# Output sums of the second pass: from loads, VectorE additions and stores to ScalarE copies and adding DMAs

## The chip, the cores and the metric

The kernel runs on one core of one Trainium2 chip. The metric is the device time of one execution in microseconds (us). Beside a few timed runs there is one profiled execution, whose trace the rows below are from. TensorE (PE, with its weight loads PEld) does the matrix products, VectorE (DVE) and ScalarE (ACT) work on tiles, GpSimd (POOL) can do the same and can issue DMAs, SyncE (SP) issues DMAs.

## The reference

A linear attention over 8 batches, 8 heads, 576 positions and head size 64 gives x with 4608 tokens and 512 features. Behind it stands a gated product without a nonlinearity, in float32:

```python
a = x @ w_a                 # 4608 x 512  @  512 x 1536
b = x @ w_b
return (a * b @ w_out)      # 1536 x 512
```

Outputs are summed over the 1536 hidden features, so the sum can be built in pieces. The change lies in the second half only.

## The kernel before, in words

Everything is kept transposed, features on partitions and tokens along the row. Each float32 operand is split into a high and a low part (`hh`, `hl`), and each product takes three matmuls.

The 1536 hidden features are done in three passes of four slices of 128 (`SLICES`). Pass 0 (`moe_block`) runs beside the attention and puts its output sums in DRAM (`parts[0]`). Passes 1 and 2 (`later_passes`) go over the tokens in blocks `t0` of up to 1024, in halves of `W` = 512: for pass 1 the blocks start at 0, 512, 1536, 2560 and 3584, the first of 512 tokens. "Second pass" is pass 1. It adds its output to pass 0's sums and puts the result in `parts[1]`, which pass 2 reads, adds to and writes to `out`.

In a block of pass 1, `winograd` first makes the hidden features with seven products per pair of slices (the keys `w11`, `s1`, `s2`, `w12`, `s3`, `w22`, `s4`) in PSUM tiles `pa..`, `pb..`. ScalarE copies some of these out of PSUM (line 691: tiles `top`, `more`, `low`), which frees the PSUM tile for the next product; VectorE adds and multiplies. Then `outputs` makes eight output tiles of 128 features by 512 tokens, `(cc, half)` = (0,0), (0,1), (1,0), ... (3,1), each of 12 matmuls (line 917) into a PSUM tile `po`. When the last of the 12 is in, line 922 loads the old sums into one of three SBUF buffers `o`, line 923 adds on VectorE, line 924 stores. The PSUM tiles of `cc` 1 and 2 are the same banks that the next block's winograd uses (`sum_ba`, `sum_bb`, `sum_ca`, `sum_cb`), so its products into `pab`, `pbb`, `pac`, `pbc` wait until these tiles are read out.

Beside this runs the decoding of pass 2's weights (`load_factors`): raw words come by DMA (`raw_..`), ScalarE scales them (line 437), VectorE assembles them, ScalarE and VectorE split them (line 150 and 157, tiles `ws_..`), and SP stores the parts (`wd_..`, line 492). The split parts have four buffers, so a fifth cast waits for the store of the first.

Each engine takes its instructions in one order, set at build time by a scheduler that sorts instructions by modelled times and readiness. So the place of an instruction in its engine's order can move although its line did not.

Of the kernel before, what the change touches and what calls it, by code (L numbers as in the profile page):

```python
# [9 lines left out]
F32 = mybir.dt.float32  # L10
# [3 lines left out]
ALU = mybir.AluOpType  # L14
# [4 lines left out]
P = 128  # L19
# [41 lines left out]
def tile_kernel(ctx, tc, qT, km, kr, vm, vr, w_phi, w_a, w_b, w_out, out):  # L61
# [13 lines left out]
    nc = tc.nc  # L75
# [3 lines left out]
    DM, NT = out.shape  # L79
# [9 lines left out]
    dpool = ctx.enter_context(tc.tile_pool(name="dpool", bufs=1, space=DRAM))  # L89
# [5 lines left out]
    xun = [dpool.tile([DM, S], F32, name=f"xun{b}") for b in range(B)]  # L95
    den = [dpool.tile([H, S], F32, name=f"den{b}") for b in range(B)]
    rec = [dpool.tile([H, S], F32, name=f"rec{b}") for b in range(B)]
    parts = [dpool.tile([DM, NT], F32, name=f"part{i}") for i in range(2)]
    xnorm = dpool.tile([DM, NT], F32, name="xnorm")


# [52 lines left out]
    def split(hi, lo, src, eng_hi, eng_lo):  # L154

        copy(eng_hi, hi, src)
        eng_lo.tensor_tensor(lo, src, hi, op=ALU.subtract)  # L157
# [425 lines left out]
    def moe_block(j):  # L583
        p, T, pool = 0, TS[0], xpool
        xs = first_x if j == 0 else list(load_x(j, pool))
        hs = []
        late = len(pools_moe) > 1

        def sums(name):

            if not late:
                return ps_moe.tile([P, T], F32, tag="moe", name=name)
            return sum_tile(next(places), name)

        places = itertools.cycle(("aa", "ab", "ca", "cb", "ba", "bb"))
        yield
        for f in range(NFS[p]):
            if f == 1:
                for c, x_ in enumerate(xs):
                    nc.sync.dma_start(xnorm[c * P : (c + 1) * P, j * T : (j + 1) * T], x_[2])  # L600
            u = f"{p}_{j}_{f}"
            pab = {}
            for nm in "ab":
                acc = sums(f"p{nm}_{u}")
                hi, lo = (weights[(p, f, nm, part)] for part in "hl")
                k = 0
                for cc in range(NCC):
                    xh, xl = xs[cc][:2]
                    for w, x in ((hi, xh), (hi, xl), (lo, xh)):
                        nc.tensor.matmul(acc, w[:, cc * P : (cc + 1) * P], x, start=(k == 0), stop=(k == 3 * NCC - 1))  # L610
                        k += 1
                pab[nm] = acc
            h32 = pool.tile([P, T], F32, tag="h32", bufs=2, name=f"h32_{u}")
            nc.scalar.copy(h32, pab["a"])  # L614
            nc.vector.tensor_tensor(h32, pab["b"], h32, op=ALU.mult)  # L615
            hh = pool.tile([P, T], F32R, tag="hh", bufs=NFS[p], name=f"hh_{u}")
            hl = pool.tile([P, T], F32R, tag="hl", bufs=NFS[p], name=f"hl_{u}")
            split(hh, hl, h32, nc.scalar, nc.vector)
            hs.append((hh, hl))
            yield  # L620
        cols = slice(j * T, (j + 1) * T)
        dst = parts[0].rearrange("(c p) s -> p c s", p=P)[:, :, cols]
        for cc in range(NCC):
            if cc % 2 == 0:
                o = pool.tile([P, 2, T], F32, tag="o", bufs=2, name=f"o_{p}_{j}_{cc}")
            acc = sums(f"po_{p}_{j}_{cc}")
            k = 0
            for f, (hh, hl) in enumerate(hs):
                hi, lo = (weights[(p, f, "o", part)] for part in "hl")
                for w, h in ((hi, hh), (hi, hl), (lo, hh)):  # L630
                    nc.tensor.matmul(acc, w[:, cc * P : (cc + 1) * P], h, start=(k == 0), stop=(k == 3 * NFS[p] - 1))  # L631
                    k += 1
            nc.scalar.copy(o[:, cc % 2], acc)
            yield
            if cc % 2:
                nc.sync.dma_start(dst[:, cc - 1 : cc + 1], o)
# [43 lines left out]
    def sum_tile(k, name):  # L680
        return pools_moe[-1].tile([P, T2 // 2], F32, tag=f"sum_{k}", name=name)
# [200 lines left out]
    def later_passes(xin, after):  # L882

        W = T2 // 2
        blocks = []
        for p, sizes in ((1, [W] + [T2] * (NT // T2)), (2, [T2] * (NT // T2) + [W])):
            t0 = 0
            for T in sizes:
                blocks.append((p, t0, T))
                t0 += T  # L890
            assert t0 == NT
        xs = yield from factors_of_x(*blocks[0], xin)
        left, old_places = None, {}
        for at, (p, t0, T) in enumerate(blocks):
            pool = pools_late[0]
            if t0 == 0:
                mine = [(pool, "o", W, 3)] * 3
                old_places[p] = itertools.cycle(mine)
            src, dst = (t.rearrange("(c p) s -> p c s", p=P) for t in (parts[p - 1], out if p == 2 else parts[1]))
            hs, acc, done = {}, {}, {}  # L900

            def outputs(cc, half, fs, p=p, t0=t0, pool=pool, src=src, dst=dst, hs=hs, acc=acc, done=done):

                key = cc, half
                if key not in acc:
                    name = f"po_{p}_{t0}_{cc}"
                    if cc in (0, NCC - 1):
                        acc[key] = ps_moe.tile([P, W], F32, tag="moe", name=f"{name}_{half}")
                    else:
                        acc[key] = sum_tile("bc"[cc - 1] + "ab"[half], f"{name}_{half}")  # L910
                tok = slice(half * W, (half + 1) * W)
                for f in fs:
                    n = done[key] = done.get(key, 0) + 1
                    hi, lo = (weights[(p, f, "o", part)] for part in "hl")
                    for i, (w, h) in enumerate(((hi, hs[f][0]), (hi, hs[f][1]), (lo, hs[f][0]))):
                        n_ = dict(start=(n == 1 and i == 0), stop=(n == NFS[p] and i == 2))
                        nc.tensor.matmul(acc[key], w[:, cc * P : (cc + 1) * P], h[:, tok], skip_group_check=True, **n_)  # L917
                if done[key] == NFS[p]:
                    cols = slice(t0 + half * W, t0 + (half + 1) * W)
                    home, tag, n, bufs = next(old_places[p])  # L920
                    o = home.tile([P, n], F32, tag=tag, bufs=bufs, name=f"o_{p}_{t0}_{cc}_{half}")[:, :W]
                    nc.sync.dma_start(o, src[:, cc, cols])
                    nc.vector.tensor_tensor(o, acc[key], o, op=ALU.add)
                    nc.sync.dma_start(dst[:, cc, cols], o)

            nq = NFS[p] // 2
            if p == 2:
                found, first, steps, last_product = out_winograd(t0, T, pool, xin, src, dst)
            else:
                found = halves_found(p, T, f"{p}_{t0}", pool, hs)  # L930
            order = [(cc, half) for cc in range(NCC) for half in range(T // W)]
            last_of_pass = t0 + T == NT
            for q in range(nq):
                low_home = (xin, "ws", 2) if (p, q) == (2, 1) else (pool, "low", 1)
                quad = winograd(p, q, T, xs, f"{p}_{t0}_{q}", pool, low_home, found)
                for _ in range(3):
                    next(quad)
                    yield
                if q == 0 and left is not None:
                    left()  # L940
                if q > 0 and p == 2:
                    first()
                elif q > 0:
                    for key in order[: T // W]:
                        outputs(*key, range(2 * q))
                next(quad)
                after(p, last_of_pass, q)
                yield
            if at + 1 < len(blocks):
                xs = yield from factors_of_x(*blocks[at + 1], xin)  # L950
            if p == 2:
                yield from steps()
                left = last_product
                continue
            early = range(2 * nq - 2)
            for cc, half in order[T // W :]:
                if cc < NCC - 1:
                    outputs(cc, half, early)
                    yield
            for key in order[:-1]:  # L960
                outputs(*key, range(0 if key[0] == NCC - 1 else early.stop, NFS[p]))
                yield

            def left(outputs=outputs, key=order[-1], n=NFS[p], p=p, last=last_of_pass):
                outputs(*key, range(n))
                after(p, last, None)

        left()
        yield
# [147 lines left out]
```

## Time and profile before

| | |
|---|---|
| timed runs, median of 3 | 1240.02 us (1239.19 to 1242.61) |
| profiled execution, time | 1242.13 us |
| its span, first to last instruction | 1240.4 us |
| TensorE busy | 1201.7 us, 97% |
| VectorE, ScalarE busy | 84%, 56% |
| second pass | from about 697 to 983 us of the span |

The span leaves 1.7 us of the profiled execution's time outside. That execution lies 2.1 us above the median of the runs. Matmuls are pipelined: a matmul of 512 columns is listed with 0.39 us, but the next one starts 0.227 us behind it.

### The profile page before, as it was taken

To read this page: it belongs to the slowest core of one execution; us is meant where nothing else is said; L and a number is where in the kernel's file an instruction comes from. 1 tells how busy PE (TensorE), PEld (TensorE's weight loads), DVE (VectorE), ACT (ScalarE), POOL (GpSimd) and SP (SyncE) were. 2 spreads that over 40 slices of the span, in tenths; PEclk is the share of its full clock that TensorE was granted. 3 is DMA by queue.
4 is the path that set the end of the run, shared out by engine and by line. 5 is a ranking of instruction groups with operands and counts; after the bars stand their busy time and mean duration, and the time that the engine had idled before them with its cause. 6 is when DMAs were issued, how large, how long until landed. Compare 5 with 4: busy or idle time off the path is not lost.

```text
span 1240.4 us, 18131 instructions
## 1 busy us (share of the span) xinstructions
PE 1201.7 (97%) x6345; PEld 981.9 (79%) x6345; DVE 1039.2 (84%) x1742; ACT 697.0 (56%) x1322; POOL 159.8 (13%) x68
## 2 busy tenths in 40 slices
PE   7989999999999999999899999999999999999998
PEld 4556887888888888887678888888788888888887
DVE  7998889998999899887498866888898688888686
ACT  5767777787687777777344544444445253424332
POOL 3331222321331222313000000000000000000000
PEclk9998999999999999999999999999999999999999
DMA  6763343453443534423463231747489714241322
GB/s 197 205 192 112 92 132 97 127 154 95 137 123 95 153 111 118 117 69 93 127 219 111 102 116 38 250 147 253 153 290 394 242 52 153 68 160 62 128 68 86
DMA packets 125420, 174.87 MB, mean 141 GB/s; under 512 B 34640, under 2 KB 63696, under 8 KB 125328
## 3 DMA queue, kind: packets, MB, share of 16 engines
q1 hardware_dynamic: 125328, 173.71, 44.4%
q8 instruction: 50, 0.82, 0.3%
q14 instruction: 42, 0.34, 0.1%
HBM read 115.10 MB, written 58.56 MB: 140 GB/s over the span
## 4 chain that ended last, share of the span: by engine, by line
PE 53%; DVE 24%; DMA 13%; issue 4%; ACT 4%; SPq 1%; DVEq 0%; ACTq 0%
PE po L917 6%; PE pba L705 6%; PE paa L705 6%; PE pa L610 4%; PE pb L610 4%; PE po L631 4%; PE kvps L282 4%; PE poa L810 3%; PE pn L368 3%; PE pac L705 3%; PE pbc L705 3%; DMA rb<-rec 2%; DVE kel L157 2%; DMA r<-den 2%; DMA xun<-xn 2%
## 5 line engine op out<-in xcount | busy, mean ns | idle before, releaser
L348 POOL PARTITION_ALL_REDUCE mb<-p x64 | 159.6, 2525 | 423.7 <-ACT p L339 349.7
L157 DVE TENSOR_TENSOR qel<-qe,qeh 128x1152 fp32r<-128x1152 f32 x54 | 73.5, 1360 | 8.7 <-ACT qeh L150 8.6
L238 ACT ACTIVATE ke<-kd 128x512 f32<-128x512 f32 x64 | 40.6, 634 | 52.7 <-DVE kd L230 48.3
L157 DVE TENSOR_TENSOR kel<-ke,keh 128x1024 fp32r<-128x1024 f32 x50 | 67.4, 1347 | 1.0 <-ACT keh L150 1.0
L352 ACT ACTIVATE qe<-p 128x576 f32<-128x576 f32 x64 | 43.9, 685 | 42.8 <-DVE p L349 41.7
L150 ACT CAST qeh<-qe 128x1152 fp32r<-128x1152 f32 x54 | 62.7, 1161 | 0.0
L282 PE MATMUL kvps<-keh,vaug 128*65 128x256 f32 x200 | 56.4, 282 | 6.3 <-DVE kvl L312 6.3
L610 PE MATMUL pb<-xh,w_b_h 128*128 128x512 f32 x144 | 58.4, 405 | 3.5 <-DVE h L615 2.2
L631 PE MATMUL po<-hh,w_o_h 128*128 128x512 f32 x144 | 57.6, 407 | 2.4 <-DVE h L615 2.1
L610 PE MATMUL pa<-xl,w_a_h 128*128 128x512 f32 x144 | 57.9, 402 | 1.4 <-DVE xl L157 1.4
L610 PE MATMUL pa<-xh,w_a_h 128*128 128x512 f32 x144 | 58.6, 407 | 0.3 <-ACT h L614 0.3
L610 PE MATMUL pb<-xh,w_b_l 128*128 128x512 f32 x144 | 58.7, 408 | 0.0
L631 PE MATMUL po<-hl,w_o_h 128*128 128x512 f32 x144 | 57.7, 401 | 0.7 <-DVE hl L157 0.7
L610 PE MATMUL pb<-xl,w_b_h 128*128 128x512 f32 x144 | 58.2, 404 | 0.0
L610 PE MATMUL pa<-xh,w_a_l 128*128 128x512 f32 x144 | 57.6, 400 | 0.0
L631 PE MATMUL po<-hh,w_o_l 128*128 128x512 f32 x144 | 57.0, 396 | 0.0
L917 PE MATMUL po<-hl,w_o_h 128*128 128x512 f32 x144 | 56.4, 392 | 0.0
L917 PE MATMUL po<-hh,w_o_l 128*128 128x512 f32 x144 | 56.1, 389 | 0.0
L282 PE MATMUL kvps<-keh,vl 128*64 128x256 f32 x200 | 55.8, 279 | 0.0
L282 PE MATMUL kvps<-kel,vaug 128*65 128x256 f32 x200 | 55.8, 279 | 0.0
L150 ACT CAST keh<-ke 128x1024 fp32r<-128x1024 f32 x50 | 52.6, 1051 | 2.4 <-PE kvps L282 2.2
L567 DVE TENSOR_TENSOR x<-x,rb 128x512 f32<-128x512 f32 x36 | 28.1, 783 | 29.7 <-DMA rb<-rec 28.7
(339 smaller groups left out, 3855.6 us busy)
## 6 DMA issues: line engine op xcount, KB each, us to landing
x<-xnorm SPq DMA_DIRECT2D x32, 512.0 KB
o<-part SPq DMA_DIRECT2D x61, 256.0 KB
q<-in_qT SPq DMA_DIRECT2D x32, 288.0 KB
xun<-xn SPq DMA_DIRECT2D x64, 144.0 KB
xnorm<-x SPq DMA_DIRECT2D x36, 256.0 KB
part<-o SPq DMA_DIRECT2D x18, 512.0 KB
part<-o SPq DMA_DIRECT2D x36, 256.0 KB
k<-in_km SPq DMA_DIRECT2D x32, 256.0 KB
```

Of the source, the lines that this page charges most:

```text
L150: eng.copy(dst, src)
L157: eng_lo.tensor_tensor(lo, src, hi, op=ALU.subtract)
L238: nc.scalar.activation(e[:, :, 0, :], d, AF.Exp)
L282: nc.tensor.matmul(st["kv_ps", b, pr][:width, j], v_[:, j, :width], e_[:, j], start=(left == NFULL and j == 0 and n_ == 0), stop=(left == ...
L348: nc.gpsimd.partition_all_reduce(mb, p32, P, bass_isa.ReduceOp.absmax)
L352: nc.scalar.activation(e[:, 0], p32, AF.Exp)
L368: nc.tensor.matmul(pn[: D + 1, :HALF], kv_[:, 2 * j + s, :], e_[:, s, tok], **at)
L610: nc.tensor.matmul(acc, w[:, cc * P : (cc + 1) * P], x, start=(k == 0), stop=(k == 3 * NCC - 1))
L631: nc.tensor.matmul(acc, w[:, cc * P : (cc + 1) * P], h, start=(k == 0), stop=(k == 3 * NFS[p] - 1))
L705: nc.tensor.matmul(accs[to][i], w_, x_, skip_group_check=True, **at)
L810: nc.tensor.matmul(accs[to][m], w_, x_, skip_group_check=True, **flags)
L917: nc.tensor.matmul(acc[key], w[:, cc * P : (cc + 1) * P], h[:, tok], skip_group_check=True, **n_)
```

## The change

One array `part` in DRAM takes the place of the two. Pass 1 no longer loads the old sums. ScalarE copies each finished output tile from PSUM into a buffer `o`, and a DMA issued from GpSimd's queue adds the buffer to the old sums in DRAM. Pass 2 reads `part`.

```diff
-    parts = [dpool.tile([DM, NT], F32, name=f"part{i}") for i in range(2)]
+    part = dpool.tile([DM, NT], F32, name="part")
...
-        dst = parts[0].rearrange("(c p) s -> p c s", p=P)[:, :, cols]
+        dst = part.rearrange("(c p) s -> p c s", p=P)[:, :, cols]
...
-            src, dst = (t.rearrange("(c p) s -> p c s", p=P) for t in (parts[p - 1], out if p == 2 else parts[1]))
+            src, dst = (t.rearrange("(c p) s -> p c s", p=P) for t in (part, out if p == 2 else part))
...
                     o = home.tile([P, n], F32, tag=tag, bufs=bufs, name=f"o_{p}_{t0}_{cc}_{half}")[:, :W]
-                    nc.sync.dma_start(o, src[:, cc, cols])
-                    nc.vector.tensor_tensor(o, acc[key], o, op=ALU.add)
-                    nc.sync.dma_start(dst[:, cc, cols], o)
+                    nc.scalar.copy(o, acc[key])
+                    nc.gpsimd.dma_start(dst[:, cc, cols], o, accum_op=ALU.add)
```

The order of the engines moves with it. First ScalarE, at the seam between block 1536 and block 2560 of the second pass, before: the raw words of the weights for pass 2 (`raw_2_a`, `raw_3_a`, `raw_2_b`) are scaled, `more` and `low` of block 2560 are copied out of PSUM.

```order
L437 ACTIVATE w_2q_a_9733<-raw_2_a 128x512 [waits DMAHW0_49]
L437 ACTIVATE w_2q_a_9764<-raw_3_a 128x512 [waits DMAHW1_49,Activation_49]
L691 COPY more_2560_0_9896<-paa_2560_0_9889 128x512 [waits PE_49]
L691 COPY more_2560_0_9896<-pba_2560_0_9890 128x512 [waits PE_49]
L150 CAST ws_1_a_w_9818<-w_2q_a_9753 128x256 [waits DVE_49]
L150 CAST ws_1_a_w_9823<-w_2q_a_9753 128x256 [waits DMAHW5_49]
L437 ACTIVATE w_2q_b_9926<-raw_2_b 128x512 [waits DMAHW0_49,DVE_49]
L150 CAST ws_1_a_s_9843<-ws_2q_a 128x256 [waits DMAHW6_49,DVE_49]
L691 COPY low_2560_0_9897<-paa_2560_0_9889 128x512 [waits PE_49,Activation_49]
```

The same place in the changed kernel, from the copy of output (0,1) on (DMASW names a DMA of GpSimd's queue, DMAHW one of SP's):

```order
L922 COPY o_1536_0_1_9771<-po_1536_0_1_9584 128x512 [waits DMASW2_49,PE_49]
L437 ACTIVATE w_2q_a_9751<-raw_3_a 128x512 [waits DMAHW6_49]
L922 COPY o_1536_1_0_9783<-po_1536_1_0_9711 128x512 [waits DMASW3_49,PE_49]
L922 COPY o_1536_1_1_9797<-po_1536_1_1_9723 128x512 [waits DMASW4_49,PE_49,Activation_49]
L922 COPY o_1536_2_0_9816<-po_1536_2_0_9732 128x512 [waits DMASW5_49,PE_49,Activation_49]
L150 CAST ws_1_a_w_9801<-w_2q_a_9740 128x256 [waits DVE_49]
L150 CAST ws_1_a_w_9806<-w_2q_a_9740 128x256 [waits DMAHW0_49]
L922 COPY o_1536_2_1_9835<-po_1536_2_1_9742 128x512 [waits DMASW6_49,PE_49,Activation_49]
L437 ACTIVATE w_2q_b_9906<-raw_2_b 128x512 [waits DMAHW7_49,DVE_49]
L150 CAST ws_1_a_s_9825<-ws_2q_a 128x256 [waits DMAHW2_49,DVE_49]
L922 COPY o_1536_3_0_9861<-po_1536_3_0_9848 128x512 [waits DMASW7_49,PE_49,Activation_49]
L691 COPY more_2560_0_9876<-paa_2560_0_9869 128x512 [waits PE_49]
```

The copy `more` stood right behind the scaling of `raw_3_a`; now five output copies, two casts, the scaling of `raw_2_b` and another cast stand between. Each output copy from the fourth on waits for the DMA that read its buffer three outputs earlier. Behind it, in the changed kernel:

```order
L150 CAST ws_1_a_s_9820<-ws_2q_a 128x256 [waits DMAHW1_49,DVE_49]
L691 COPY more_2560_0_9876<-pba_2560_0_9870 128x512 [waits PE_49]
L150 CAST ws_1_a_s_9839<-ws_2q_a 128x256 [waits DMAHW1_49,Activation_49]
L150 CAST ws_1_a_w_9844<-w_2q_a_9775 128x256 [waits DMAHW2_49,Activation_49]
L437 ACTIVATE w_2q_b_10015<-raw_3_b 128x512 [waits DMAHW0_49,DVE_49]
L150 CAST ws_1_b_w_10161<-w_2q_b_9958 128x256 [waits DMAHW3_49,Activation_49]
L150 CAST ws_1_a_s_9865<-ws_2q_a 128x256 [waits DMAHW4_49,Activation_49]
L691 COPY low_2560_0_9877<-paa_2560_0_9869 128x512 [waits PE_49]
```

`low` moved behind four more casts and the scaling of `raw_3_b`; the last casts wait for stores (`wd_..`) of the first ones.

TensorE, at the same seam in the changed kernel, after the 12 matmuls of output (3,0), four of the products into `paa` and `pba` (key s2), one into `pab` and six into `pac`:

```order
L705 MATMUL pab_2560_0_9873<-xgl_2560_0_9660,w_0_a_w_7934 128x512
L705 MATMUL pab_2560_0_9873<-xgh_2560_0_9659,w_0_a_w_7934 128x512
L705 MATMUL pab_2560_0_9873<-xgh_2560_1_9698,w_0_a_w_7934 128x512
L705 MATMUL pbc_2560_0_9872<-xth_2560_0_9651,w_0_b_s_8045 128x512 [waits Activation_49]
L705 MATMUL pbc_2560_0_9872<-xtl_2560_0_9652,w_0_b_s_8045 128x512
L705 MATMUL pbc_2560_0_9872<-xth_2560_0_9651,w_0_b_s_8045 128x512
L705 MATMUL pbc_2560_0_9872<-xth_2560_1_9690,w_0_b_s_8045 128x512
L705 MATMUL pbc_2560_0_9872<-xtl_2560_1_9691,w_0_b_s_8045 128x512
L705 MATMUL pbc_2560_0_9872<-xth_2560_1_9690,w_0_b_s_8045 128x512
L705 MATMUL pab_2560_0_9873<-xgl_2560_1_9699,w_0_a_w_7934 128x512
L705 MATMUL pab_2560_0_9873<-xgh_2560_1_9698,w_0_a_w_7934 128x512
L705 MATMUL pbb_2560_0_9874<-xgh_2560_0_9659,w_0_b_w_8039 128x512
```

Before, `pbc` and its neighbours waited for VectorE and came behind the s3 product into `paa`; now they wait for ScalarE, and the s3 product follows the six of `pbb`. Behind it come six into `pba`, the 12 of output (3,1), four into `pab`, and then the first w22 product into `paa`, which waits for `low`.

## Rows read from the trace of the kernel before

**Rows 1.** The page of the profile: its span, and the busy time of TensorE with share and instructions.

```profile
span 1240.4 us, 18131 instructions
PE 1201.7 (97%) x6345; PEld 981.9 (79%) x6345; DVE 1039.2 (84%) x1742; ACT 697.0 (56%) x1322; POOL 159.8 (13%) x68
```

**Rows 2.** Busy time in windows of 60 us of the second pass: the window, its length, busy us and instructions of PE, PEld, DVE, ACT, POOL, granted TensorE clock, DMA share, GB/s.

```profile
700.00:760.00 60.00, 59.14 (x326) 51.44 (x326) 42.88 (x72) 25.22 (x44) 0.00 (x0) 1.00 0.31 96
760.00:820.00 60.00, 59.52 (x262) 48.81 (x262) 49.44 (x85) 25.16 (x46) 0.00 (x0) 1.00 0.51 171
820.00:880.00 60.00, 59.41 (x261) 48.31 (x259) 51.31 (x90) 24.73 (x44) 0.00 (x0) 1.00 0.60 202
880.00:940.00 60.00, 59.88 (x263) 49.34 (x264) 52.71 (x96) 26.81 (x48) 0.00 (x0) 1.00 0.73 258
```

**Rows 3.** Waits from 690 to 1000 us: who waited for what, us in total, times, longest. First those of PE, then one of ACT, then two of SP's DMA queue.

```profile
PE pba L705 <- ACT top L691: 1.1, 2, 0.6
PE paa L705 <- ACT top L691: 0.9, 1, 0.9
...
ACT more L691 <- PE paa L705: 20.2, 9, 5.3
...
SPq L924 <- DVE o L923: 25.7, 21, 6.3
SPq L922 <- DMA part<-o: 24.0, 19, 3.9
```

**Rows 4.** Costs: the VectorE additions of line 923 as a group (busy us, mean ns, idle before); ScalarE's copies of such an output tile in pass 0 and SP's issues of the loads (times, then ns minimum/median/maximum, first and last start); GpSimd's one kind of instruction.

```profile
L923 DVE TENSOR_TENSOR o<-po,o 128x512 f32<-128x512 f32 x36 | 24.3, 684 | 8.7 <-DMA o<-part 4.8 <-PE po L917 2.7 <-PE pab L705 1.1
...
L633 ACT COPY o<-po x36: 565/587/616, 162.7 to 697.2; 128x512 f32<-128x512 f32 x36
L922 SPq DMA_DIRECT2D o<-part x36: 319/320/1339, 701.4 to 976.8; - x36
...
L348 POOL PARTITION_ALL_REDUCE mb<-p x64 | 159.6, 2525 | 423.7 <-ACT p L339 349.7
```

**Rows 5.** The chain of waits at the seam between blocks 1536 and 2560: start us, length us, what. `part`, `wd_a_w` and `o` are transfers of 256 KB.

```profile
785.49 2.24 DMA part<-o
787.75 3.76 DMA o<-part
792.74 5.91 DMA wd_a_w<-ws_a_w
800.70 4.29 DMA o<-part
```

**Rows 6.** TensorE's instructions at the same seam: start us, listed us, line. 781.13 to 782.13 are the last five matmuls of output (0,0), 787.80 is the last of (2,1), 788.93 the first of (3,0), 793.47 the first s3 product into `paa`, 802.53 the first w22 product into it.

```profile
781.13 0.48 PE L917 MATMUL po<-hl,w_o_h 128*128 128x512 f32 x1
...
782.13 0.39 PE L917 MATMUL po<-hh,w_o_l 128*128 128x512 f32 x1
...
787.80 0.39 PE L917 MATMUL po<-hh,w_o_l 128*128 128x512 f32 x1
...
788.93 0.39 PE L917 MATMUL po<-hh,w_o_h 128*128 128x512 f32 x1
...
793.47 0.39 PE L705 MATMUL paa<-xuh,w_a_s 128*128 128x512 f32 x1
...
802.53 0.39 PE L705 MATMUL paa<-xuh,w_a_w 128*128 128x512 f32 x1
```

**Rows 7.** ScalarE's instructions there; in brackets the idle time before and what ended it.

```profile
782.84 0.68 ACT L437 ACTIVATE w_2q_a<-raw_a 128x512 f32<-128x512 f32 x1 [1.58 <-DMA raw_a<-in_w_a]
787.01 0.66 ACT L437 ACTIVATE w_2q_a<-raw_a 128x512 f32<-128x512 f32 x1 [3.49 <-DMA raw_a<-in_w_a]
788.68 0.59 ACT L691 COPY more<-paa 128x512 f32<-128x512 f32 x1 [1.01 <-PE paa L705]
...
796.04 0.66 ACT L437 ACTIVATE w_2q_b<-raw_b 128x512 f32<-128x512 f32 x1 [4.69 <-DMA raw_b<-in_w_b]
796.61 0.39 ACT L150 CAST ws_a_s<-ws_2q_a 128x256 fp32r<-128x256 f32 x1
796.91 0.58 ACT L691 COPY low<-paa 128x512 f32<-128x512 f32 x1
...
804.16 0.41 ACT L150 CAST ws_a_s<-ws_2q_a 128x256 fp32r<-128x256 f32 x1 [3.10 <-DMA wd_a_s<-ws_a_s]
```

**Rows 8.** VectorE's instructions there: one step of the decoding, the first additions of line 923, the last step that reads `raw_2_a`, the fourth addition.

```profile
784.45 0.42 DVE L438 TENSOR_SCALAR w_2q_a<-w_2q_a 128x512 uint32<-128x512 uint32 x1
784.78 1.28 DVE L923 TENSOR_TENSOR o<-po,o 128x512 f32<-128x512 f32 x2
...
788.98 0.68 DVE L443 SCALAR_TENSOR_TENSOR w_2q_a<-raw_a,w_2q_a 128x512 f32<-128x512 uint32 x1
...
791.63 0.69 DVE L923 TENSOR_TENSOR o<-po,o 128x512 f32<-128x512 f32 x1 [0.43 <-DMA o<-part]
```

**Rows 9.** SP's issues there: three loads of old sums, then two of raw words (512 KB each).

```profile
787.75 1.88 SPq L922 DMA_DIRECT2D o<-part  x3
789.74 1.91 SPq L454 DMA_DIRECT2D raw_b<-in_w_b  x2
```

## The prediction

> **What bounds the kernel now.** The page comes first: TensorE is busy 97% of a span of 1240.4 us [rows 1], so time can only come out of its gaps, or go into new ones. The change touches the second pass, so next the windows of that pass [rows 2]: TensorE works 59.14, 59.52, 59.41 and 59.88 of 60 us, at a granted clock of 1.00; VectorE 43 to 53, ScalarE about 25, GpSimd nothing. All gaps together are 2.05 us. The list of waits says whose they are [rows 3]: 1.1 us in `pba` and 0.9 us in `paa`, each behind a ScalarE copy into `top`. No row has TensorE waiting for the addition of line 923 in this pass. The long waits stand on the other side: ScalarE waits 20.2 us for TensorE before it may copy `more`, so it comes early and has slack; SP waits 25.7 us for the additions and 24.0 us for the stores. These cost nothing as long as TensorE runs on.
>
> **What is taken away.** VectorE loses 36 additions of 684 ns, 24.3 us of work [rows 4]. SP loses 36 loads and 36 stores of about 0.32 us of issue each, and its waits for them. None of it is behind a gap of TensorE, so it gives back only indirectly: SP gets to later loads earlier. Of the 2.05 us the 0.9 us lie at 701.9, before the first output, and stay; the 1.1 us in `pba` may go, since the x tiles ahead of that copy come from SP's queue. Gain: 0 to 1.1 us. I take all of it.
>
> **What is added: ScalarE.** 36 copies of 0.587 us (the same copy in pass 0, [rows 4]) are 21.1 us in a pass where ScalarE is idle more than half of the time. As work that is hidden. But ScalarE takes its instructions in order, and the order printed above puts five output copies, the scaling of `raw_2_b` and three casts between the scaling of `raw_3_a` and the copy of `more`, and four more casts and another scaling ahead of `low`. TensorE needs both copies for its next products into `paa`. So the price depends on two latencies: that of the adding DMA (the fourth output copy waits until the first buffer is free) and that of the raw words.
>
> **What is added: the adding DMA.** Call L the time from the end of a copy until its buffer is free again. The trace has no DMA from GpSimd and none that adds. The bounds, by the nearest rows: below, SP's issue of 0.32 us [rows 4] and a lone store of 256 KB in 2.24 us [rows 5], 2.6 us. Above, GpSimd's only instruction, 2.53 us [rows 4], for the issue, then a slow load (4.29) and a slow store (5.91) one after the other [rows 5], 12.7 us. I take 1.3 us for the issue, near the middle of 0.32 and 2.53, and 4.0 us for the transfer: it must read the old sums, which took 3.76 us in this place, and its 128 rows can be written while others are read. L = 5.3 us.
>
> The Trainium skill, DMA: Bandwidth & Descriptors, section Anatomy of one DMA, gives a plain DMA from GpSimd about 2.0 us and its bytes at 436 GB/s, an estimate of 2.6 us for 256 KB; it says nothing of adding. No row here shows such a DMA. By it L would be 2.6, the lower case below.
>
> **The seam, step by step.** I lay the new orders on the times of before, at the seam between the blocks 1536 and 2560. TensorE ends (0,0) at 782.5 (782.13 + 0.39), and then one output every five matmuls of 0.227: (0,1) 783.7, (1,0) 784.8, up to (2,1) at 788.2 (787.80 + 0.39) [rows 6]. ScalarE copies (0,0) until 783.2 and (0,1) until 784.3. Then it is held by `raw_3_a`, which comes at 787.0 and takes 0.66 [rows 7]; (1,0) is copied until 788.3. (1,1) needs the buffer of (0,0), free at 783.2 + L = 788.5: done 789.1. (2,0) needs that of (0,1): done 790.2. (2,1) needs that of (1,0): 788.3 + L + 0.6 = 794.2.
>
> TensorE starts (3,0) at 788.0, right behind (2,1), and is through at 790.8; four matmuls and one bring it to 791.9, `pac` to 793.2, three of `pab` to 793.9. There `pbc` needs the bank of (2,1): it waits 0.3 us, in general L - 5.0. Then `pbc`, two of `pab`, six of `pbb`, 14 x 0.227: the s3 product is due at 797.1 + 0.3 = 797.4.
>
> Before it, ScalarE must scale `raw_2_b`. These words came at 796.0 [rows 7]; their load was issued from 789.74 [rows 9], when VectorE was through with `raw_2_a` [rows 8], and took 6.3 us behind three loads of old sums that had just been issued. Those loads are gone, adding DMAs take their place; VectorE reaches `raw_2_a`'s last step no earlier, because it waits for `raw_3_a`. I take one us earlier, 795.0, between no gain and the 2 us by which 768 KB less would be felt. Then 0.66 for the scaling, 0.4 for the cast, 0.6 for copying (3,0), whose buffer is free at 789.1 + L = 794.4, and `more` out at 797.3: in time, by a hair. With the words at 796.0 it is 0.9 us late.
>
> Then `low`. The cast behind `more` ends about 797.7, VectorE's part of it 0.4 later, and its store, issued by 798.5, lands at 804.4 if it takes 5.91 [rows 5], at 800.7 if 2.24. A cast that needs this buffer, then `low`: 801.7 to 805.4. Before, that cast did wait 3.10 us for such a store, and ran at 804.16, but behind `low`, which was out at 796.91 [rows 7]. TensorE wants it 28 matmuls after the s3 product began, at 797.4 + 6.3 = 803.7. Late by 0 to 1.7; I take 0.9.
>
> Sum for a seam: 0.3 + 0.2 + 0.9 = 1.4 us. The seams behind the blocks 512, 1536 and 2560 carry a decoding of weights; 3 x 1.4 = 4.2. Block 0 has four outputs, one of which waits for a buffer, and block 3584 no decoding; I take 0 for both. With the gain of 1.1: **+3.1 us**. On the profiled execution that is 1242.1 + 3.1 = 1245.2. It lay 2.1 above the median of the runs, so for the median I forecast 1243.1.
>
> Pass 2 reads `part` instead of `parts[1]`. In both orders its first reads wait for the last writes, and the first sum it needs was loaded ten us ahead of its use; the order of the rest is the same. Nothing for it.
>
> **Rivals.** A measurement of this kernel can tell about 0.3%, 3.7 us, from no change.
>
> *All hidden (0.24).* L under 4.5 and `raw_2_b` two us earlier: `pbc` has its bank, `more` is 1 us early, `low` on time within 0.4. Speaks for it: a lone store took 2.24 us, and ScalarE is half idle. 0 to 1.2 for the seams less 1.1: 1239 to 1240.
>
> *Slow adding (0.22).* One mechanism: the adding DMA takes longer than a load, because it reads, adds and writes behind one another while weights and raw words use the same engines (DMA share 0.51 to 0.73 [rows 2]). It decides from about L = 7. At L = 8: `pac` waits 1.0, `pbc` 2.0 more, (3,0) is copied until 800.4 and `more` 0.9 late, `low` 1.7: 5.6 a seam, with block 3584 four of them, 22 us: 1261. At 12.7, with the same steps, 15 a seam, about 1300. Speaks for it: 5.91 us for one store there [rows 5]. Against: three transfers in flight at most.
>
> *GpSimd held up by VectorE (0.04).* The decoding has single-input VectorE steps that run in 0.42 us where two-input ones of the same size take 0.68 [rows 8]. If GpSimd cannot write its list of transfers beside them, L grows by up to 0.42: `pbc` 0.4 more at three seams, +1.3, 1244.4. SBUF — State Buffer in the Trainium skill, section Who interferes with whom, states that lock; no row here shows it, since GpSimd is idle in this pass.
>
> *Faster by over 0.3% (0.03).* TensorE's gaps here are too small; it would need a shorter matmul pitch or the gaps of another pass.
>
> The forecast itself has 0.47: +0.5 to +6.5 us, half of it beyond 3.7 or nearly so.
>
> **Chances and range.** Slower by over 0.3%: 0.20 of the 0.47, the 0.22, and 0.03 of the lock: 0.45. Same: 0.27 + 0.24 + 0.01 = 0.52. Faster: 0.03. The likeliest case alone (0.47) gives 1240.5 to 1246.5. The range takes in "all hidden" below, and above the slow adding up to L about 7.3 (17 us): 1238.5 to 1257. What is left out is most of the slow case and a little below.
>
> **What would show it.** In the changed profile: line 922 on ScalarE 36 times at 0.59 us; TensorE's idle time in the second pass 4 to 7 us, ended by ScalarE, in `pbc` by a copy of `o`, in `paa` by `more` or `low`; ScalarE waiting for `part<-o` and for `raw_b` just before. The chain of waits should pass through line 923's DMA. If ScalarE shows no wait for `part<-o`, L is short and the first step is wrong. If each seam costs over 4 us, and `pac` too waits, L is 7 or more. If TensorE's gaps are unchanged and the time still moves, the reasons lie outside the pass, and this sum is void.

## The result, and the profile after

The changed kernel takes 1254.75 us (median of six runs, 1252.64 to 1257.41), the kernel before 1241.58 on the same chip (six runs, 1239.19 to 1243.57). The ratio is 1.0106, 95% interval 1.0094 to 1.0119: slower by about 13 us. The forecast was 1243.1, with 1238.5 to 1257.0 as its range; the likeliest case alone (1240.5 to 1246.5) does not hold the result. The profiled execution took 1253.94 us, its span 1252.2.

The page of the changed kernel, busy times, the group of GpSimd's DMAs, and the second pass in windows (columns as in [rows 2]):

```profile
PE 1206.1 (96%) x6345; PEld 983.0 (79%) x6345; DVE 1018.7 (81%) x1706; ACT 715.9 (57%) x1358; POOL 190.6 (15%) x104
...
L923 POOL DMA_DIRECT2D part<-o x36 | 31.7, 922 | 384.3 <-ACT o L922 377.7
```

```profile
700.00:760.00 60.00, 59.28 (x322) 51.42 (x323) 40.05 (x66) 27.69 (x49) 3.69 (x4) 1.00 0.26 62
760.00:820.00 60.00, 55.03 (x234) 44.23 (x233) 42.65 (x78) 26.25 (x49) 6.99 (x8) 0.97 0.58 154
820.00:880.00 60.00, 58.70 (x256) 47.50 (x255) 42.69 (x74) 27.10 (x48) 6.98 (x8) 1.00 0.58 148
880.00:940.00 60.00, 57.44 (x250) 46.15 (x249) 46.52 (x80) 29.21 (x51) 7.11 (x8) 1.00 0.61 181
```

Against [rows 2] TensorE has lost time in three of four windows, and in 760 to 820 its granted clock fell to 0.97. VectorE is relieved as planned (1018.7 us over the whole span, against 1039.2 in [rows 1]). The first product of the pass stands at 701.94 before and at 700.59 after, the spans end at 1240.4 and 1252.2: from there to the end the changed kernel takes 13.1 us more. All of it falls in the second pass, for a cast of the third pass, `hh_w<-low`, is as late (1024.92 against 1013.15, 11.8 us) as the span's end (11.8 us).

The waits of the second pass, 700 to 1010 us (columns as in [rows 3]):

```profile
PE pba L705 <- DVE low L732: 4.9, 2, 2.9
PE paa L705 <- ACT low L691: 2.5, 2, 1.6
PE paa L705 <- ACT top L691: 1.1, 1, 1.1
PE paa L705 <- ACT more L691: 0.7, 2, 0.4
PE po L917 <- DVE hl L157: 0.6, 1, 0.6
PE pba L705 <- ACT low L691: 0.4, 1, 0.4
PE pbc L705 <- DVE more L695: 0.4, 1, 0.4
PE pbc L705 <- ACT o L922: 0.4, 1, 0.4
```

```profile
ACT o L922 <- DMA part<-o: 27.2, 17, 5.4
...
ACT more L691 <- PE paa L705: 6.5, 5, 2.1
```

The 1.1 us in `pba` behind `top` are gone, as forecast. In place of three waits there are eleven, in eight rows; of these only `paa` behind `top` was there before. ScalarE's slack ahead of `more` fell from 20.2 [rows 3] to 6.5 us; it now waits 27.2 us for the adding DMAs. The largest new row, 4.9 us in two waits, was in no sum of mine. Of the 11.0 us of all rows ScalarE ends 5.1 and VectorE 5.9; the forecast had waits behind ScalarE alone.

The seam of the forecast's rows. It is the one between the blocks 512 and 1536, and not, as the rows and the forecast name it, between 1536 and 2560: the windows above have four DMAs on GpSimd (block 0) before 760, so the outputs copied from 782.45 are those of block 512. ScalarE's order there is the one printed for the later seam, so the steps of the forecast hold for it as they stand. ScalarE (compare [rows 7]; everything is 1.1 us earlier here), then TensorE (compare [rows 6]), then VectorE:

```profile
782.45 1.06 ACT L922 COPY o<-po 128x512 f32<-128x512 f32 x2
...
786.31 0.57 ACT L922 COPY o<-po 128x512 f32<-128x512 f32 x1
787.60 0.59 ACT L922 COPY o<-po 128x512 f32<-128x512 f32 x1 [0.72 <-DMA part<-o]
789.45 0.59 ACT L922 COPY o<-po 128x512 f32<-128x512 f32 x1 [1.27 <-DMA part<-o]
...
791.72 0.59 ACT L922 COPY o<-po 128x512 f32<-128x512 f32 x1 [1.07 <-DMA part<-o]
793.39 0.66 ACT L437 ACTIVATE w_2q_b<-raw_b 128x512 f32<-128x512 f32 x1 [1.08 <-DMA raw_b<-in_w_b]
...
795.52 0.59 ACT L922 COPY o<-po 128x512 f32<-128x512 f32 x1 [1.18 <-DMA part<-o]
796.00 0.59 ACT L691 COPY more<-paa 128x512 f32<-128x512 f32 x1
...
799.86 0.41 ACT L150 CAST ws_a_s<-ws_2q_a 128x256 fp32r<-128x256 f32 x1 [2.48 <-DMA wd_a_w<-ws_a_w]
...
804.30 0.58 ACT L691 COPY low<-paa 128x512 f32<-128x512 f32 x1
```

```profile
796.64 0.50 PE L705 MATMUL paa<-xuh,w_a_s 128*128 128x512 f32 x1 [0.44 <-ACT more L691]
...
804.93 0.50 PE L705 MATMUL paa<-xuh,w_a_w 128*128 128x512 f32 x1 [1.60 <-ACT low L691]
...
816.80 0.80 PE L705 MATMUL pba<-xfh,w_b_w 128*128 128x512 f32 x1 [2.92 <-DVE low L732]
...
820.28 0.62 PE L705 MATMUL pac<-xth,w_a_s 128*128 128x512 f32 x2
```

```profile
813.24 0.69 DVE L661 TENSOR_TENSOR xs<-x,xs 128x512 f32<-128x512 f32 x1 [2.50 <-DMA x<-xnorm]
...
816.06 0.68 DVE L732 TENSOR_TENSOR low<-pba,low 128x512 f32<-128x512 f32 x1
```

`more` is late by 0.44 us and `low` by 1.60, at the steps where the forecast had them late (0.2 and 0.9). Then comes a third wait: TensorE needs the bank `pba`, line 732 on VectorE frees it, and ahead of line 732 VectorE's list has lines 661 and 662, which wait for an x load. Behind the 2.92 us of idling eight matmuls, 816.80 to 820.28, take 3.48 us in place of 8 x 0.227 = 1.82.

### The profile page after: what moved, and what is told of

Read it like the earlier page. It is cut to its first block, busy times and chain, and to the rows that moved or that the text cites. A ratio compares the mean times of both kernels' runs of the same rounds, so it can differ in the third digit from the quotient of the medians.

```text
span 1252.2 us, 18103 instructions
## 1 busy us (share of the span) xinstructions
PE 1206.1 (96%) x6345; PEld 983.0 (79%) x6345; DVE 1018.7 (81%) x1706; ACT 715.9 (57%) x1358; POOL 190.6 (15%) x104
## 3 DMA queue, kind: packets, MB, share of 16 engines
q0 software_dynamic: 5184, 9.44, 4.9%
## 4 chain that ended last, share of the span: by engine, by line
PE 48%; DVE 22%; issue 13%; DMA 12%; ACT 2%; POOL 1%; SPq 1%; DVEq 0%; POOLq 0%; ACTq 0%
PE po L631 5%; PE pa L610 5%; PE pb L610 5%; PE kvps L282 4%; PE paa L705 4%; PE pba L705 4%; PE pn L368 4%; PE poa L810 3%; PE po L917 2%; DMA rb<-rec 2%; PE pk L226 2%; PE pac L705 2%; PE pbc L705 2%; PE pq L337 2%; DMA r<-den 2%
## 5 line engine op out<-in xcount | busy, mean ns | idle before, releaser
L923 POOL DMA_DIRECT2D part<-o x36 | 31.7, 922 | 384.3 <-ACT o L922 377.7
```

## The experiments

Three theories; C was formed after the first four runs, so the expectations of these name A and B alone. **A:** the order; lines 661 and 662 ahead of 732 make the cost. **B:** the output buffers come free late, and ScalarE holds up what stands behind its copies. **C:** the adding DMAs hold the DMA engines, and the transfers of the decoding and of x land late, whoever waits for what. Ratios are to the kernel before on the same chip, with 95% intervals.

**The order on VectorE.** `freed` keeps the steps of line 732; the scheduler is told to put two steps behind the one of the block that runs. Apart from their neighbours nothing moves.

```diff
 nc.vector.tensor_tensor(t2, x12, x11, op=ALU.subtract)
-nc.vector.tensor_tensor(t1, x22, t2, op=ALU.subtract)
-nc.vector.tensor_tensor(t3, x22, x12, op=ALU.subtract)
+with tc.issue_after(freed[-2].ins) if p == 1 and c == 0 and t0 > 2 * T2 else ExitStack():
+    nc.vector.tensor_tensor(t1, x22, t2, op=ALU.subtract)
+    nc.vector.tensor_tensor(t3, x22, x12, op=ALU.subtract)
```

> The changed kernel, in which two VectorE steps on the next block's x (lines 661 and 662, first pair, blocks 2560 and 3584) are put behind line 732's step of the block that runs; nothing else is moved by hand. Theory A (the order on VectorE: lines 661 and 662 stand ahead of line 732 and wait for an x load, so TensorE waits 2.92 and 1.96 us in pba, and its next eight matmuls run at half clock, about 1.7 us): those stalls go, 6 to 7 us less, about 1248 against 1254.75; the stalls in paa and pbc (0.2 to 1.6 us, some 4 us together) stay. Theory B (the adding DMA is slow, buffers come free late, and any order would stall): the 4.9 us come back elsewhere, 1252 to 1255.

Measured: 1.0088 (1.0068 to 1.0108). The longest of TensorE's waits in the pass are now these (`pbb` behind VectorE has 0.9 us, once):

```profile
PE paa L705 <- ACT low L691: 2.0, 2, 1.0
PE pac L705 <- DVE more L695: 1.6, 2, 1.2
```

The 4.9 us in `pba` are gone and no window's clock is below 1.00, but new waits stand in `pac` and `pbb`. By the ratios some 2 us come back, which the intervals do not part from nothing; the 6 to 7 us that A expected would be a ratio of about 1.005 and lie outside the interval. A falls as the main cause: the long wait was where the lateness showed, not what made it.

**No adding.** The same DMA from GpSimd's queue as a plain store, which leaves the addition of the old sums out; in the second pass every engine's list stays the same.

```diff
-nc.gpsimd.dma_start(dst[:, cc, cols], o, accum_op=ALU.add)
+nc.gpsimd.dma_start(dst[:, cc, cols], o)
```

> The changed kernel with a plain store from GpSimd's queue in place of the adding one (the old sums are not added, so part of the computation is left out); the order on every engine is that of the changed kernel. Theory B (adding makes the DMA long): landing falls from 6.3 us to 3 or 4, ScalarE's 27 us of waiting for part<-o to under 10, the stalls in paa and pbc go, and because the decoding comes earlier those in pba shrink too: 1243 to 1248. Theory A with issue and transfer as the main cost: landing stays above 5 us, ScalarE still waits over 20 us, the stalls stay, 1252 to 1255.

Measured: 1.0008 (0.9994 to 1.0023): nearly the whole loss is gone, with the new order still in place. The profiled execution was the slowest of the ten (1248.93 us against a median of 1246.05), and 2.5 of the 4.9 us in `pba` behind line 732 still stand in it. GpSimd's DMAs by their line: issues (ns minimum/median/maximum, first and last start) and time to landing, in the changed kernel and then here:

```profile
L923 POOL DMA_DIRECT2D part<-o x36: 862/872/1231, 730.7 to 997.5; - x36
...
DMA to landing us min/median/max: 3.9/6.3/9.2
```

```profile
L923 POOL DMA_DIRECT2D part<-o x36: 539/539/693, 737.4 to 992.5; - x36
...
DMA to landing us min/median/max: 2.3/3.1/7.5
```

The DMA queues from 700 to 1010 us (q1 is SP's, q0 GpSimd's; packets, MB, share of 16 engines), in the same order:

```profile
q1 hardware_dynamic: 20520, 40.21, 38.2%
q0 software_dynamic: 5184, 9.44, 19.9%
```

```profile
q1 hardware_dynamic: 21600, 42.74, 41.1%
q0 software_dynamic: 2880, 9.44, 8.0%
```

For the same 9.44 MB the adding holds the DMA engines 2.5 times as long: 0.199 x 310 / 36 = 1.71 us of all sixteen for each 256 KB, against 0.69. SP's queue, q1, needs about as much per MB in both (0.95% and 0.96%). The wait of ScalarE for `part<-o` fell from 27.2 to 7.5 us, so this run alone does not part B from C.

**Copies on VectorE.** `nc.vector.tensor_copy` in place of `nc.scalar.copy`.

> The changed kernel with the output copies on VectorE in place of ScalarE; the adding DMA stays. VectorE waits for the buffers now, and its new order has line 732 ahead of lines 661 and 662. Theory A (order): more and low are copied on time, no pba stall over 1 us, 1243 to 1247. Theory B (slow adding, whoever copies): VectorE waits 20 to 30 us for part<-o, decoding and the releases of pab, pbb, pac behind it come late, 1250 to 1258.

Measured: 1.0046 (1.0029 to 1.0064). VectorE waits 14.8 us for `part<-o`, about half of what ScalarE did. There is no wait behind line 732, but `paa` still waits 4.8 us for `low`, with ScalarE free of output copies. Neither A's nor B's expectation holds in full. C, formed later, fits it, but so would a mixture of A and B.

**Five output buffers.**

```diff
-mine = [(pool, "o", W, 3)] * 3
+mine = [(pool, "o", W, 3)] * 3 + [(extra, "stage", DM, 2)] * (2 if p == 1 else 0)
...
-for pool, tag, n in itertools.cycle(((extra, "stage", DM), (xin, "raw", 2 * DM))):
-    yield lambda name: pool.tile([P, n], F32R, tag=tag, bufs=2, name=name)[:, :DM]
+while True:
+    t = xin.tile([P, 2, DM], F32R, tag="raw", bufs=2, name="ws_pair")
+    for i in range(2):
+        yield lambda name, i=i: t[:, i]
```

> The changed kernel with five output buffers in place of three in the second pass (two taken from the staging of decoded weights, which uses both halves of the tag raw instead). Lines 661 and 662 still stand ahead of line 732. Theory B (buffers come free late): ScalarE waits for part<-o under 10 us, the stalls in paa and pbc go, and with earlier decoding the x load too: 1243 to 1247. Theory A (order): the 4 us in paa and pbc may go, the pba stalls of 2 to 3 us with their slow clock stay at two seams: 1248 to 1252.

Measured: 1.0091 (1.0076 to 1.0106). ScalarE waits 1.2 us for `part<-o` in place of 27.2, and nothing is won:

```profile
ACT w_2q_b L437 <- DMA raw_b<-in_w_b: 11.5, 3, 4.6
```

It waits for raw words instead, and `paa` 4.5 us for `low`. B falls as the main cause. (The pairs that the casts now share also free their buffers later, so a part of these waits may be the edit's own.)

**Adding DMAs that nobody waits for.** Outputs go out as plain stores from SP. Behind each of 28 stores GpSimd adds (first run) or stores (second run) 256 KB of output weights, which lie ready in SBUF, to the same place. What is added are not the old sums, so both kernels leave that step of the computation out. The two have the same list on every engine in the second pass.

```diff
-nc.gpsimd.dma_start(dst[:, cc, cols], o, accum_op=ALU.add)
+nc.sync.dma_start(dst[:, cc, cols], o)
+if t0 < 3584:
+    w = weights[(p, cc, "o", "h")].bitcast(F32)
+    nc.gpsimd.dma_start(dst[:, cc, cols], w, accum_op=ALU.add)
```

> Output copies on ScalarE and plain stores from SP, so no buffer waits for an adding DMA. Behind each store (not in the last block) GpSimd adds 256 KB of output weights, which lie ready in SBUF, to the same place in DRAM, 28 times; no engine waits for these in the pass (what is added is not the old sums, so the computation is changed). Theory C (the adding DMA keeps the DMA engines busy, and raw words, decoded weights and x land late): slower than the same kernel with a plain store in its place by 5 to 10 us. Theory B (only the output buffers that come free late matter): the two kernels agree within 2 us.

> The kernel of the run before with a plain store in place of the adding one behind each output's store: same order on all engines, same bytes named, no addition (the computation is changed). Theories B and C: about as the changed kernel with plain stores, 1.000 to 1.003 of the kernel before.

Measured: 1.0067 (1.0044 to 1.0089) with the adding, 0.9991 (0.9976 to 1.0007) with the plain store. Some 9 us for 28 transfers for which no engine waits in the pass: that is C, and B's agreement within 2 us is excluded. (They come on top of the stores, so the 9 us are not a part of the 13.) Where it bites is seen in ScalarE's waits for raw words, 700 to 1010 us, first with the adding, then with the plain store (the waits of `ws_b_w` for the stores `wd_a_s` fall from 8.1 to 3.3 us in the same way):

```profile
ACT w_2q_b L437 <- DMA raw_b<-in_w_b: 13.7, 4, 5.3
```

```profile
ACT w_2q_b L437 <- DMA raw_b<-in_w_b: 3.3, 2, 1.7
```

And at the seam behind block 512, by time: SP's issue of the first `raw_b` and ScalarE's read of it, in the same order:

```profile
794.61 0.38 SPq L454 DMA_DIRECT2D raw_b<-in_w_b  x1
...
804.28 0.66 ACT L437 ACTIVATE w_2q_b<-raw_b 128x512 f32<-128x512 f32 x1 [4.27 <-DMA raw_b<-in_w_b]
```

```profile
791.66 0.38 SPq L454 DMA_DIRECT2D raw_b<-in_w_b  x1
...
797.53 0.66 ACT L437 ACTIVATE w_2q_b<-raw_b 128x512 f32<-128x512 f32 x1 [1.67 <-DMA raw_b<-in_w_b]
```

From issue to read this load takes 9.7 us beside the adding DMAs and 5.9 beside plain ones.

**One array.** The kernel before with `[dpool.tile([DM, NT], F32, name="part")] * 2`.

> The kernel before with one array of sums in place of two, nothing else; the order on every engine stays. Theories A, B and C: no change, within 0.2% of the kernel before.

Measured: 0.9992 (0.9975 to 1.0009). This part of the change costs nothing.

**Half of the adding.** `accum_op=ALU.add if half == 0 else ALU.bypass`: 20 of the 36 DMAs add, the other 16 store and leave the old sums out.

> The changed kernel in which the outputs of the second half of each block are stored plainly by GpSimd, 16 of 36 (their old sums are left out), the other 20 added as before; order as in the changed kernel. Theory C (each adding DMA takes its share of the DMA engines): about half of what the adding costs, 1.004 to 1.006 of the kernel before. Theory A (order alone): as the changed kernel, 1.009 or more.

Measured: 1.0066 (1.0042 to 1.0090), between none (1.0008) and all (1.0106). In proportion, 20 of 36 would be 1.0062.

**Rows of 2 and of 4 KB.** As the adding nobody waits for, but from `xnorm` in DRAM: 28 DMAs of 256 KB, or, for both halves of a block at once, 4 of 256 and 12 of 512 KB.

```diff
+old = xnorm.rearrange("(c p) s -> p c s", p=P)
+nc.gpsimd.dma_start(dst[:, cc, cols], old[:, cc, cols], accum_op=ALU.add)
```

> As the run with adding DMAs that nobody waits for, but what is added lies in DRAM (xnorm) in place of SBUF; rows of 2 KB, 28 DMAs (the computation is changed). Orders on all other engines stay. Theory C with the adding itself as the slow step: GpSimd's queue takes about as much of the DMA engines as with the source in SBUF (20% of their time in the pass for 28 DMAs is 15 to 16%), 1.005 to 1.009 of the kernel before.

> The kernel of the run before with rows of 4 KB: 4 DMAs of 256 KB and 12 of 512 KB in place of 28, the same bytes added. If the time on the DMA engines goes by packets, the queue's share halves and the loss falls to about half, 1.002 to 1.005. If it goes by bytes, share and loss stay, 1.005 to 1.009.

Measured: 1.0082 (1.0063 to 1.0101) and 1.0039 (1.0026 to 1.0051). GpSimd's queue in the kernel with adding from SBUF, and then with rows of 4 KB, 700 to 1010 us:

```profile
q0 software_dynamic: 4032, 7.34, 15.0%
```

```profile
q0 software_dynamic: 2304, 7.34, 13.4%
```

The share of the engines' time goes nearly by bytes, not by packets (2304 against 4032 for the same 7.34 MB); and yet the loss halves. Fewer and later adding DMAs in a seam may be the reason. So may the order: unlike the kernel with rows of 2 KB, this one has moved steps in the second pass's lists of ScalarE, VectorE and SP. Neither was tried apart; it stays open.

**The decoding moved by 8 steps,** earlier (-10 in place of -18 in `due`) and later (-26).

> The changed kernel with the decoding of the third pass's weights begun 8 steps earlier (-10 in place of -18), so that it is spread over four seams in place of three. Theory C (the adding DMAs collide with the decoding's transfers in the seams): fewer transfers in a seam, the loss falls to 1.003 to 1.008. Theory B (buffers): no difference to the changed kernel, 1.009 to 1.012.

> The changed kernel with that decoding begun 8 steps later (-26). Theory C: in each seam one or two raw tiles come after the outputs in place of among them, the loss falls to 1.004 to 1.009, unless the last weights come too late for the third pass. Theory B: 1.009 to 1.012.

Measured: 1.0137 (1.0104 to 1.0170) and 1.0146 (1.0126 to 1.0165): slower both ways, which no theory had. No run shows what these shifts do without adding DMAs, so they part nothing.

## Why the range held and the forecast did not

**Gain.** 1.1 us were to come from `top` in `pba`; that wait is gone. Right.

**L.** In the seam the buffers of (0,0), (0,1), (1,0) and (1,1), copied by 783.0, 783.5, 786.9 and 788.2, were written again from 787.60, 789.45, 791.72 and 795.52: L = 4.6, 5.9, 4.8, 7.3, mean 5.7. (Over the pass, from issue to landing, the DMAs take 3.9 to 9.2, in the median 6.3.) I took 5.3; the issue is 0.87 us (1.3 taken), the rest longer. Right in size.

**The three waits of a seam.** Forecast 0.3 in `pbc`, 0.2 for `more`, 0.9 for `low`, 4.2 in three seams. Measured in the whole pass: 0.4, 0.7 and 2.5 + 0.4, together 4.0. Right in the sum; the single waits came out unequal. `low` came to 1.6 in this seam because the store `wd_a_w` took 9.0 us (790.89 to 799.86) where the slowest row had 5.91 [rows 5]. One step was misread without effect: ScalarE scales the first `raw_a` ahead of the copy of (0,0), which by [rows 7] would end at about 784.0 and not 783.2; no wait of the sum hangs on it.

**What failed** is the step "Sum for a seam": it ends at `low`. The rest of the block came after: 4.9 us in `pba`, 1.7 at the lower clock, 1.0 in `po` and `pbc` behind VectorE. With the net 3.1 forecast this makes 10.7 of the 13.1. The rest lies around each wait, where the rows count as busy what is not. The last matmul before 804.93 starts at 802.94; less the pitch of 0.227 that is a wait of 1.77 us where the row has 1.60. And the matmul behind 804.93 starts at 805.27, 0.34 us later in place of 0.227. That is some 0.27 us for each of eight more waits, about 2 in all.

**Why the range held.** Its upper end was set for slow adding with L at about 7.3 and a wait in `pac` at every seam. That case did not come, so it is by luck that the range reached far enough.

The reason lies deeper than where the sum stops. I priced an adding DMA by its latency alone and never by the time for which it holds the DMA engines, 1.71 us for 256 KB. Over the pass this is hidden. Before, 700 to 1010 us:

```profile
q1 hardware_dynamic: 31382, 60.22, 56.8%
```

After, the queues hold 38.2 + 19.9 = 58.1%. So the sum over the pass cannot be the cause; it was nearly as high before and cost nothing. In the 16 us of the seam from two us after the first `raw_a` issue, the queues moved, before and then after:

```profile
DMA packets 3114, 4.15 MB, mean 259 GB/s; under 512 B 195, under 2 KB 2002, under 8 KB 3112
...
q1 hardware_dynamic: 3112, 4.12, 79.0%
```

```profile
q0 software_dynamic: 631, 1.16, 51.0%
q1 hardware_dynamic: 1869, 1.87, 37.5%
```

Half of the engines' time goes to 1.16 MB of adding. SP's share falls from 79.0 to 37.5%, but mostly because the loads and stores of sums are gone from its queue: before, 3112 - 2002 = 1110 packets of 2 KB were 2.27 of its 4.12 MB, and the 1.85 MB left are as much as the 1.87 after. So in this stretch the raw words are not late against the kernel before: the first `raw_b` is scaled 4.9 us behind its issue (788.46 to 793.39), before 6.3 [rows 7, rows 9].

What the adding makes late shows beside the kernel with the plain store, whose lists are the same. ScalarE there, at the same seam:

```profile
788.88 1.05 ACT L922 COPY o<-po 128x512 f32<-128x512 f32 x2
...
799.44 0.67 ACT L437 ACTIVATE w_2q_b<-raw_b 128x512 f32<-128x512 f32 x1 [2.70 <-DMA raw_b<-in_w_b]
...
803.91 0.41 ACT L150 CAST ws_a_s<-ws_2q_a 128x256 fp32r<-128x256 f32 x1 [1.75 <-DMA wd_a_w<-ws_a_w]
...
807.38 0.58 ACT L691 COPY low<-paa 128x512 f32<-128x512 f32 x1
```

Counted from the first output copy (782.45 and 788.88), with adding and then without: `raw_b` is scaled at 10.9 and 10.6 us, `more` copied at 13.6 and 11.9, `low` at 21.9 and 18.5, and line 732 starts at 33.6 and 29.4. The raw words give 0.4 of these 4.2 us. About 1.3 come at the output copies that wait for buffers, 1.7 more by `low`, where the stores of decoded weights take 9.0 us in place of 7.2 (796.67 to 803.91), and the rest behind it, where line 661 waits 2.50 us for x in place of 1.09. The 2.92 us of TensorE ahead of 816.80 are 1.55 there. The lateness adds up along the decoding, and TensorE meets it where a step that waits for a transfer stands ahead of a bank's release. When one such place is taken away (the order), or the wait for buffers, other waits appear, as those two runs show. That the engines' time, and not something else about an adding DMA, is what delays the other transfers is argued from the shares; no run tells them apart. I had the row for the suspicion: the share of the DMA engines in [rows 2].

**The rivals.** "Slow adding" named the engines, but as what makes the adding slow, from L = 7, with waits in `pac` at every seam. The adding is slow (6.3 us to landing against 3.1 plain), but L stayed at 5.7 in this seam and `pac` did not wait: that path to the loss is not what the runs show. "All hidden" is excluded by the three waits. The lock by VectorE: GpSimd's issues took 0.87 us in the median, seven of the 36 between 0.92 and 1.23; at most 0.4 us more, as the rival had it, and whether VectorE was the reason is not shown. The wait in `pbc` that it was to lengthen at three seams is 0.4 us in the whole pass. The formula cited in the forecast (the Trainium skill, DMA: Bandwidth & Descriptors, Anatomy of one DMA), an estimate of 2.6 us, lies near the plain store from GpSimd's queue (2.3 at least, 3.1 in the median); the adding DMA, of which that section says nothing, took 6.3.

## What to carry to other kernels

Price a DMA twice: its latency for whoever waits, and the time for which it holds the DMA engines for everybody else, in the stretch where it runs and not over the span. A DMA that adds is not a store for free: here it cost the engines somewhat more than the load and the store that it replaced (1.71 us against 2 x 0.77, from q1's 56.8% for 60.22 MB). All of it falls when the data is ready, while a load can run ahead; that this timing makes the loss is argued here, not tried apart. To find out whether a transfer hurts by being waited for or by being there, run it as a bystander that nobody waits for, beside a plain one of the same size.

## What the runs showed of the hardware

An adding DMA held all sixteen DMA engines for 1.71 us per 256 KB (153 GB/s), a plain store of the same queue for 0.69 (380 GB/s). It took 144 packets (5184 for 36) against 80. GpSimd's issue of it took 0.87 us in the median, against 0.54. From issue to landing it took 6.3 us in the median, against 3.1.

TensorE's granted clock fell after some waits and not after others, and the length of the wait alone does not sort them. In the changed kernel, behind 2.92 us of idling, eight matmuls ran at a pitch of 0.43 us, the 1.2 GHz level, and then again at 0.227, the 2.4 GHz level. With five buffers it fell behind a wait of 2.34 us, with half of the adding behind one of 1.98 (the windows 760 to 820 and 880 to 940 show 0.97). Behind 1.96 us in the changed kernel, 2.37 with the copies on VectorE and 2.46 with the adding that nobody waits for, the windows show 1.00.
